# One written-out order of all steps replaced by another in an attention and Fourier-mixing kernel

## The chip, the core and the metric

The kernel runs on one core of a Trainium2 chip. The core has a matrix engine (PE, with its weight loads shown as PEld), a vector engine (DVE), a scalar engine (ACT), GpSimd (POOL) and a queue engine (SP) that here only starts transfers. Each engine works through its own list of instructions in the order in which the program gave them; between engines, semaphores hold an instruction back until what it reads is there and what it overwrites has been read. Transfers are started from SP, a few from ACT and POOL, and run on 16 DMA engines. The metric is the device time of the kernel in microseconds (us); lower is better.

## The reference, cut to what matters

Inputs are q, k and v of shape (4 batches, 8 heads, 768 positions, 64), and two matrices of 512x2048 and 2048x512. For each batch and head:

```python
k_rep = k.reshape(B, H, 12, 64, D).mean(axis=3)             # 12 blocks of 64 keys
gate = einsum('bhsd,bhnd->bhsn', q, k_rep), causal blocks only
sel = the 3 best blocks of each row, and its own block
scores = q @ k.T / 8, kept where the block is selected and the key is not later
attn_out = softmax(scores) @ v
```

The heads are put side by side to x of shape (4, 768, 512), and then

```python
mixed = real(fft(fft(x, axis=1), axis=2))
u = x + mixed
un = (u - mean(u)) / sqrt(var(u) + 1e-6)
out = u + maximum(un @ w_ch1, 0) @ w_ch2                    # 512 -> 2048 -> 512
```

## The kernel before, in words

Work on attention is cut into 16 pairs of heads, P = 0 to 15; batch b holds the pairs 4b to 4b+3. What follows works on a whole batch, in tiles of 128 positions.

The program is a list of steps, the string `ORDER` (line 112). A loop at its end (line 884) takes one word after another and calls the function that `WORK` (line 863) has for it. Since the tile framework runs with a manual schedule for all five engines, each engine's list is exactly the order in which these words put instructions on it. A word reads `name:numbers@place`. The place chooses which buffer of several a tile gets: for results of PE one of four pairs of PSUM banks (0 to 3), for loads one of two or three buffers in SBUF. A `~` ahead of the word gives its evacuation or copy to the other engine of two.

The steps that the prediction speaks of, by name, with their functions:

- `Lk`, `Lq`, `Lv` load k, q, v of a pair from SP (`load`, four transfers for k or q of pairs 7 and up at line 297, two before that at line 302, one for v at line 289). `LT` and `LF` load the Fourier tables fs_sb and fd_sb. `W`, `X` load the two matrices from POOL's queue. `Lc`, `Li` load the block indicators.
- `tk`, `tq` transpose k and q on PE, for pairs 0 to 6; `kb` and `qc` do it on DVE for the later ones. `ks`, `kh` sum blocks of keys (DVE); `kc`, `qc`, `qs` copy to 16 bits (`~qs` on ACT instead of POOL).
- `g` scores blocks on PE; `gt`, `gx`, `go`, `gl`, `gm` find the third-best block on DVE; for pairs from 7 on, `K` writes the mask into the operand on POOL.
- `s:P,i` computes the i-th of six tiles of scores on PE, `e:P,i` its exponential on ACT, `d:P,i` the causal diagonal on POOL.
- `vc` casts v (POOL, with `~` ACT), `v:P` multiplies with v on PE, `x:P` divides on DVE and writes x.
- `fs`, `fd`, `f` fold x by the symmetries of the Fourier sums (DVE); `y:b,h` and `m:b,kp` are the two Fourier products on PE. `ty` copies y on ACT (`~ty`: DVE), `tr` copies it reversed on DVE (`~tr`: ACT). `u` adds x and mixed (DVE). `xu` writes the 16-bit rows of u (ACT, `~xu`: DVE). `xt` transposes them on PE and `un` copies the result to unT on DVE, for batch 0; for the batches 1 to 3 `un` is two transposing transfers from SP (line 660). `bn`, `nv`, `nr` make the statistics.
- `w:b,it` multiplies unT with one of 16 column tiles of the first matrix, on PE; `r` is the relu that evacuates it (ACT, line 731, or with `~` DVE, line 729). `c` is the second product, `o` adds it to u (DVE), `od` stores.
- For batch 3 the second product is done by a seven-product scheme: `S` (`h_comb`) and `T` combine the operands on DVE, `p` multiplies, `po` adds to u.

A stage of one batch is laid among those of the next: the products `w` and `c` of batch b stand between the scores and exponentials of the pairs of batch b+1.

Of the kernel before, what the change touches and what calls it, by code (L numbers as in the profile page):

```python
# [117 lines left out]
gl:2 d:1,4 gt:3 vc:0 e:1,1 s:1,0@1 ~kc:4 tq:4@0 d:0,5 Lv:1@0 e:1,0 s:1,2@2 d:0,2 gx:3 v:0@3 Lk:5@2
e:1,2 gm:2@2 d:1,0 go:3 gl:3 gm:3@3 ~qc:4@1 s:1,5@1 s:2,4@2 vc:2 x:0 Lk:7@0 e:1,5 s:2,5@0 d:1,1
s:2,1@1 e:2,5@0 d:1,3 e:2,4 tq:5@3 fs:0,1 d:1,5 vc:1 g:4@0 e:2,1 qc:5@0 s:2,0@2 d:1,2 gt:4 e:2,0  # L120
s:2,2@3 Lq:6@0 d:2,4 d:2,5 s:2,3@1 fs:0,0 tk:5@0 e:2,2 qs:5 gx:4 v:1@2 go:4 Lv:3@1 ks:5 e:2,3 kb:7
kc:5 s:3,5@3 s:3,3@1 d:2,3 d:2,2 Lv:5@0 e:3,5@1 gl:4 s:3,4@0 d:2,1 e:3,3 x:1 g:5@3 qs:4 Lq:7@1
e:3,4 s:3,0@1 gt:5 d:2,0 s:3,2@2 d:3,3 fs:1,0 s:3,1@3 e:3,0 vc:3 gx:5 v:2@0 ks:7 e:3,1 d:3,4 d:3,5
# [12 lines left out]
s:7,5@2 w:0,14@1 Lv:7@0 e:7,5 e:7,4 kh:9 qc:9@1 Lq:10@1 s:7,1@2 X:0 r:0,10 go:8 ~r:0,14 w:0,0@3
e:7,1 d:7,4 gl:8 gm:8@0 K:8 s:7,3@0 ~r:0,0 g:9@1 e:7,3 w:0,15@2 bn:0,5 kb:10 w:0,2@3 r:0,15 X:1
fs:4,1 kc:8 ks:10 d:7,1 s:7,0@0 vc:7 v:6@2 gt:9 kc:9 gx:9 qs:9 w:0,4@1 ~r:0,2 e:7,0 go:9 d:7,3
w:0,9@3 gl:9 d:7,5 gm:9@1 ~r:0,4 d:7,0 K:9 s:8,2@0 Lk:11@1 x:6 v:7@1 e:8,2@0 bn:0,4 r:0,9 s:8,3@2
w:0,13@0 fs:5,0 e:8,3 x:7 s:9,0@3 fs:6,0 s:9,5@2 nv:0 w:0,7@1 e:9,5@1 ~r:0,13 e:9,0 nr:0 s:9,2@2  # L140
fs:4,0 r:0,7 kh:10 fs:7,1 s:8,1@0 fs:7,0 s:8,0@3 e:9,2 fs:6,1 c:0,0,0@1 fd:6,0 qc:10@0 e:8,0 fd:7,0
# [11 lines left out]
K:12 bn:1,1 e:10,2 g:13@0 fs:8,1 w:1,15@1 gt:13 s:11,1@0 d:10,2 ~r:1,15 w:1,13@3 d:10,5 e:11,1
d:10,1 ~r:1,9 vc:11 s:10,4@1 kb:14 r:1,13 d:11,0 w:1,0@0 Lv:12@0 vc:10 e:10,4 kb:15 d:10,3 s:11,5@2
s:12,0@3 ks:14 d:10,0 e:11,5 Lv:15@1 w:1,1@1 kc:13 d:10,4 d:11,5 od:0,2 gx:13 d:11,1 d:11,3 v:10@2
~r:1,1 r:1,0 qs:13 ~vc:12 go:13 s:12,3@0 w:1,8@1 fs:9,0 Lv:13@0 e:12,3@1 qc:14@1 gl:13 w:1,6@0
kh:14 ks:15 r:1,8 e:12,0 fs:8,0 w:1,7@1 bn:1,2 r:1,6 x:10 vc:13 s:12,1@3 r:1,7 s:12,2@0 gm:13@1
v:11@2 Lv:14@0 e:12,1 fs:10,1 K:13 od:0,4 e:12,2 g:14@1 w:1,4@3 gt:14 x:11 s:13,3@0 r:1,4 w:1,2@1
bn:1,5 bn:1,0 w:1,11@2 r:1,2 fs:10,0 fd:10,0 e:13,3@0 s:13,1@3 ~r:1,11 s:12,4@1 e:13,1 w:1,3@0
fd:10,1 gx:14 e:12,4 w:1,12@2 fs:11,0 r:1,3 nv:1 go:14 gl:14 nr:1 fs:11,1 s:13,0@3 kh:15 r:1,12  # L160
s:12,5@1 c:1,0,0@0 e:12,5 e:13,0 s:13,5@2 g:15@1 e:13,5 s:13,2@3 d:13,0 gt:15 c:1,1,0 d:13,5 e:13,2
fd:11,1 d:12,2 fd:11,0 kc:15 gx:15 w:1,14@2 gm:14@2 go:15 f:2,2 K:14 s:13,4@1 f:2,3 r:1,14 c:1,0,1
f:2,1 kc:14 gl:15 f:2,0 y:2,1@3 ~qs:15 y:2,0@2 d:13,3 ~tr:2,1 d:13,1 d:12,1 qs:14 c:1,1,1 e:13,4
tr:2,0 ty:2,0 d:13,4 c:1,4,0@1 d:12,4 o:1,1 d:12,0 ~ty:2,1 od:1,1 d:13,2 od:0,3 m:2,2@2 gm:15@3
o:1,0 m:2,0@3 K:15 od:1,0 v:13@0 u:2,0@0 c:1,4,1 u:2,2@1 d:12,3 pg:2 d:12,5 s:15,4@3 x:13 v:12@2
e:15,4@0 o:1,4 s:14,4@0 ~xu:2,2 s:14,1@3 e:14,4@1 un:2,2 c:1,5,0 fs:13,1 x:12 e:14,1 bn:2,4
s:15,3@0 d:14,1 d:15,4 s:15,0@2 e:15,3 ~xu:2,0 s:15,5@3 c:1,5,1 un:2,0 fs:13,0 e:15,0 d:15,3 e:15,5
m:2,1@0 s:15,2@2 u:2,1@4 c:1,2,0@3 e:15,2 bn:2,2 d:15,2 xu:2,1 d:14,4 s:14,5@0 s:14,2@2 o:1,5
un:2,1 c:1,2,1 e:14,5 d:15,0 bn:2,0 e:14,2 ~vc:15 c:1,3,0 od:1,4 s:14,0@1 c:1,3,1 e:14,0 ~vc:14
d:14,0 w:2,14@0 o:1,2 o:1,3 od:1,2 s:15,1@2 bn:2,1 od:1,3 w:2,1@1 e:15,1 od:1,5 ~r:2,14 d:15,1  # L170
# [749 lines left out]
```

## Time and profile before

| | |
|---|---|
| median of 3 runs | 285.47 us (283.56 to 288.51) |
| the profiled execution's own time | 282.36 us |
| span in its profile, first to last instruction | 280.6 us |
| PE busy | 270.4 us (96%) |
| DVE busy | 221.4 us (79%) |
| ACT busy | 166.3 us (59%) |
| POOL busy | 105.3 us (38%) |
| moved by DMA | 33.45 MB in 121280 packets |

The span is what the profile shows from the first instruction to the last; the rest of the time lies around it. Busy time of PE counts the pipelined matmuls with their modelled ends, so that neighbours overlap: two steps that follow without a gap start closer together than one matmul is long. The chain of work that ended last is followed back from the end, from each instruction to what released it or to its predecessor on the engine. A wait is idle time of an engine, put down to the semaphore that came last.

### The profile page before, as it was taken

The page shows a single profiled execution, that of the slowest core. Times are in us where ns is not written, and L with a number is a line of the kernel's source. Part 1 is how long each engine was busy: PE and PEld are TensorE (multiplying, and loading weights), DVE is VectorE, ACT ScalarE, POOL GpSimd, SP SyncE. Part 2 cuts the span into 40 slices and gives each one's busy share as a digit, 9 for nine tenths or more (in the row PEclk, how much of TensorE's full clock was granted, in tenths as well). Part 3 has the DMA queues.
Part 4 walks back from the last instruction along what each step waited for, and adds up shares of the span by engine and source line. Part 5 has one row for each costly group of instructions (what it writes and reads, how often), then busy time and mean ns, then how long its engine had stood idle before and what let it go on. Part 6 is the DMA issues. An engine that isn't in the chain of part 4 may idle for free.

```text
span 280.6 us, 6763 instructions
## 1 busy us (share of the span) xinstructions
PE 270.4 (96%) x2581; PEld 173.5 (62%) x2581; DVE 221.4 (79%) x683; ACT 166.3 (59%) x205; POOL 105.3 (38%) x273
## 2 busy tenths in 40 slices
...
GB/s 192 263 228 196 208 225 191 213 195 93 164 195 180 149 207 192 113 138 166 179 124 0 1 73 43 77 75 114 0 2 0 0 49 140 1 89 27 0 2 262
DMA packets 121280, 33.45 MB, mean 119 GB/s; under 512 B 113760, under 2 KB 118304, under 8 KB 121248
## 3 DMA queue, kind: packets, MB, share of 16 engines
...
q10 hardware_dynamic: 1712, 0.40, 0.7%
...
HBM read 28.55 MB, written 6.29 MB: 124 GB/s over the span
## 4 chain that ended last, share of the span: by engine, by line
PE 87%; DVE 4%; DMA 4%; SPq 2%; issue 1%; ACT 0%; ACTq 0%; DVEq 0%
PE c L738 22%; PE h L719 20%; PE h L721 10%; PE sc L457 7%; PE cw L794 7%; PE av L492 6%; PE yp L562 2%; SPq L297 2%; PE tp L317 2%; PE mx L595 2%; PE sc L452 2%; PE mx L596 2%; DMA fd_sb<-c_FD 2%; DMA nat<-in_q_dram 2%; PE g L378 1%; PE sc L464 1%
## 5 line engine op out<-in xcount | busy, mean ns | idle before, releaser
L474 ACT ACTIVATE pt<-sc 128x1024 f16<-128x1024 f32 (+1 forms) x96 | 83.8, 918 | 27.4 <-PE sc L457 22.3
L719 PE MATMUL h<-unT,w 128*128 128x512 f16 x256 | 84.8, 379 | 0.0
L721 PE MATMUL h<-unT,w 128*128 128x256 f16 x256 | 69.7, 272 | 0.0
L738 PE MATMUL c<-w_sb,hT 128*128 128x512 f16 x288 | 65.4, 379 | 0.0
L480 POOL TENSOR_SCALAR_AFFINE_SELECT pt<-pt 128x256 f16<-128x256 f16 x96 | 38.6, 427 | 44.1 <-ACT pt L474 38.7
L731 ACT ACTIVATE hT<-h 128x768 f16<-128x768 f32 x39 | 30.9, 810 | 38.1 <-PE h L721 38.1
L738 PEld LDWEIGHTS <-hT 128*128 128x128 f16 x288 | 27.8, 98 | 31.1
L719 PEld LDWEIGHTS <-w 128*128 128x128 f16 x256 | 25.0, 98 | 29.1 <-issue 0.9
L729 DVE TENSOR_SCALAR hT<-h 128x768 f16<-128x768 f32 x25 | 23.6, 946 | 10.0 <-PE h L721 9.9
L251 POOL TENSOR_SCALAR_AFFINE_SELECT qk<-mt 32x160 f16<-32x160 f16 x72 | 24.2, 357 | 15.3 <-DVE mt L429 13.3
L721 PEld LDWEIGHTS <-w 128*128 128x128 f16 x256 | 25.0, 98 | 3.6
L457 PE MATMUL sc<-qk 96*128 96x512 f16 (+3 forms) x144 | 26.5, 306 | 0.0
L492 PEld LDWEIGHTS <-pt 128*128 128x128 f16 x672 | 22.4, 97 | 2.4 <-POOL pt L480 0.4
L492 PE MATMUL av<-v,pt 128*128 128x65 f16 x672 | 23.3, 193 | 0.1
L744 DVE SCALAR_TENSOR_TENSOR u<-c,rs,u 128x512 f32<-128x512 f32 x18 | 13.0, 743 | 9.6 <-PE c L738 9.6
L457 PEld LDWEIGHTS <-qk 96*128 96x128 f16 x144 | 13.1, 97 | 9.2 <-issue 0.8
L614 DVE SCALAR_TENSOR_TENSOR u<-mx,x 128x512 f32<-128x512 f32 x22 | 14.3, 685 | 5.6 <-PE mx L596 5.4
L251 POOL TENSOR_SCALAR_AFFINE_SELECT qk<-q 64x768 f16<-64x768 f32 (+1 forms) x17 | 14.2, 834 | 8.3 <-ACT q L237 8.0
L248 DVE TENSOR_TENSOR x<-av,rcp 128x768 f16<-128x768 f32 x16 | 15.3, 958 | 0.5
L251 POOL TENSOR_SCALAR_AFFINE_SELECT v<-nat 128x768 f16<-128x768 f32 x12 | 10.9, 905 | 12.8 <-DMA nat<-in_v_dram 12.7
L452 PE MATMUL sc<-qk 64*128 64x512 f16 (+3 forms) x112 | 14.7, 306 | 0.8 <-ACT pt L474 0.6
L343 ACT CAST qk<-nat 64x768 f16<-64x768 f32 x18 | 14.9, 830 | 0.4
(132 smaller groups left out, 401.9 us busy)
## 6 DMA issues: line engine op xcount, KB each, us to landing
...
```

The source lines that it names most:

```text
L251: nc.gpsimd.affine_select(out=out, in_=in_, pattern=[[0, i] for i in n], base=0, channel_multiplier=0, compare_op=ALU.is_ge, fill=0.0)
L452: nc.tensor.matmul(ps[:, e, co:co + q1 - q0], qk[hs[e], 1, XW(P), 128 * jt:128 * jt + 128], qk[hs[e], 0, XW(P), q0:q1], start=(co == 0), s ...
L457: nc.tensor.matmul(ps[:, e, co:co + q1 - q0], qk[0:96, e, 1, 128 * jt:128 * jt + 128], qk[0:96, e, 0, q0:q1], start=True, stop=True)
L474: nc.scalar.activation(out=d["pt"][:, o:o + 2 * n].rearrange("p (e c) -> p e c", e=2), in_=d["sc", i][:, :, 0:n], func=AF.Exp, scale=0.125)
L480: nc.gpsimd.affine_select(out=dg, in_=dg, pattern=[[0, 2], [1, 128]], base=0, channel_multiplier=-1, compare_op=ALU.is_ge, fill=0.0)
L492: nc.tensor.matmul(av[:, e, 66 * st:66 * st + 65], pt[:, co:co + 128], vv[:, e, jt, 0:65], start=(cnt == 0), stop=(cnt == 20))
L719: nc.tensor.matmul(hp[:, 0:512], w1s, unT[:, dt, 0:512], start=(dt == 0), stop=(dt == NDT - 1))
L721: nc.tensor.matmul(hp[:, 512:768], w1s, unT[:, dt, 512:768], start=(dt == 0), stop=(dt == NDT - 1))
L729: nc.vector.tensor_scalar(out=hT, in0=hp, scalar1=0.0, scalar2=None, op0=ALU.max)
L731: nc.scalar.activation(out=hT, in_=hp, func=AF.Relu)
L738: nc.tensor.matmul(c_ps[b, g[0]][:, st - g[0], :], h_t[b, it][:, 128 * st:128 * (st + 1)], w2_sb[:, it, :], start=(it == 0), stop=(it == N ...
L794: nc.tensor.matmul(o, x, y, start=(i == 0 and W7_FIRST[n]), stop=(i == 7), skip_group_check=True)
```

## The change

The 1058 words of `ORDER` stay the same set of steps; their order is another, and so are 250 of the places behind `@`: 78 of `s`, 51 of `w`, 22 of `e`, 15 of `v`, the others in smaller numbers. Also changed is which steps carry the `~`:

- relus: 25 with `~` (on DVE) before, 18 after; ten get it and seventeen lose it
- `kc:0`, `kc:2` go to DVE and `kc:4` to ACT
- `qs:7`, `qs:9`, `qs:14` go to ACT, `qs:10` and `qs:12` to POOL
- `vc:4`, `vc:7`, `vc:9`, `vc:10`, `vc:13` go to ACT, `vc:14` and `vc:15` to POOL
- `tr:0,0`, `tr:1,0`, `tr:3,1` go to ACT, `tr:2,1` to DVE; `ty:0,1`, `ty:2,0`, `ty:3,1` go to DVE
- `xu:0,1` and `xu:2,1` go to DVE, `xu:2,0` and `xu:2,2` to ACT

In `h_comb` the two operands of a step are looked up only when that step runs, instead of all four ahead; this lets an `S` step stand ahead of a relu that it does not read, and changes no instruction.

The parts of the diff that the text below speaks of, with the lines between them left out:

```diff
 ORDER = """
...
-fs:2,0 e:4,4@0 fs:2,1 fd:2,1 e:4,1 Lv:4@1 gm:5@1 s:4,5@1 s:5,2@3 x:3 e:4,5 s:5,5@2 e:5,2@1 s:4,0@1
-Lk:9@2 d:4,5 fs:1,1 s:4,2@0 fs:3,1 e:4,0 fs:3,0 s:5,0@3 fd:2,0 fd:3,0 e:5,5 s:4,3@1 e:4,2 fd:3,1
-s:5,4@2 kh:7 f:0,1 e:5,4 s:5,3@0 f:0,0 LF:0 e:5,0 tk:6@2 f:0,3 e:4,3 Lk:8@1 f:0,2 y:0,0@3 ks:6 pg:0
-d:4,2 e:5,3 d:5,0 qc:7@1 W:1 y:0,1@1 kc:6 d:4,4 tr:0,0 Lq:8@2 g:6@0 d:4,0 ~tr:0,1 d:5,4 gt:6 vc:4
-m:0,2@2 ty:0,1 gx:6 W:0 s:5,1@0 ty:0,0 go:6 gl:6 u:0,2@0 g:7@1 d:5,3 qs:6 e:5,1 m:0,1@3 gt:7 ~vc:5
-d:5,1 m:0,0@2 u:0,1@1 d:4,1 xu:0,2 d:4,3 v:4@0 W:2 gm:6@2 xu:0,1 u:0,0@2 s:6,5@1 s:6,3@3 Lc:0
-e:6,5@0 e:6,3 xt:0,1@2 ~xu:0,0 s:6,1@1 un:0,1 xt:0,2@3 d:6,3 e:6,1 qs:7 xt:0,0@2 un:0,2 s:6,4@1
-un:0,0 s:6,2@3 e:6,4 kb:8 d:5,2 w:0,8@2 d:5,5 d:6,5 gx:7 w:0,5@1 go:7 x:4 r:0,8 e:6,2 gl:7 s:6,0@2
...
-d:8,5 od:0,1 g:11@3 Lq:13@2 g:12@0 ~qs:11 gt:11 m:1,1@2 gx:11 c:0,4,1 kc:12 go:11 gl:11 gm:11@3
-un:1,2 K:11 c:0,2,0@3 xu:1,0 o:0,5 gt:12 kb:13 c:0,3,0 od:0,5 u:1,1@2 d:9,0 un:1,0 d:9,1 d:8,0 vc:9
-s:11,4@0 s:11,2@2 o:0,4 c:0,3,1 xu:1,1 d:9,4 qc:15@0 un:1,1 pg:1 v:8@1 o:0,3 gx:12 c:0,2,1 e:11,4@0
...
+v:3@1 fs:2,1 Lv:4@0 W:0 e:4,0 gl:5 fd:2,0 LF:0 gm:5@1 ~qc:6@1 s:4,5@3 fs:1,0 s:5,0@0 x:3 e:4,5
+s:5,2@2 e:5,0@1 d:4,5 s:4,2@3 Lv:5@1 fs:1,1 s:5,5@1 e:4,2 fs:3,1 s:4,1@0 fs:3,0 fd:2,1 e:5,5 fd:3,0
+s:4,3@3 e:4,1 s:5,3@1 fd:3,1 f:0,0 e:5,2 tk:6@0 e:5,3 f:0,1 s:5,4@2 f:0,2 e:4,3 Lk:8@2 y:0,0@1
+f:0,3 ks:6 e:5,4 d:4,3 d:4,2 ks:7 d:4,0 ~tr:0,0 g:6@3 qs:6 y:0,1@2 gt:6 ty:0,0 d:5,4 gx:6 W:1
+s:5,1@3 Lc:0 ~tr:0,1 go:6 m:0,2@1 gl:6 W:2 kh:7 gm:6@2 kc:6 ~ty:0,1 Lk:9@1 d:4,1 ~vc:4 d:5,3
+m:0,0@0 u:0,2@0 d:5,5 e:5,1 d:5,0 d:4,4 m:0,1@2 u:0,0@1 xu:0,2 d:4,3 v:4@1 u:0,1@2 s:6,5@3 s:6,1@0
+e:6,5@0 e:6,1 s:6,0@3 s:6,3@2 ~xu:0,0 e:6,0 ~xu:0,1 xt:0,0@0 un:0,0 e:6,3 xt:0,1@3 xt:0,2@0 un:0,1
+kc:7 g:7@2 un:0,2 s:6,2@3 gt:7 s:6,4@0 e:6,2 gx:7 w:0,8@2 ~vc:5 go:7 x:4 d:6,2 d:5,1 w:0,1@3 r:0,8
+d:6,3 gl:7 d:5,2 gm:7@3 ~qs:7 pg:0 kb:8 d:6,0 w:0,6@1 Lq:8@2 K:7 bn:0,4 w:0,11@2 r:0,6 bn:0,2 r:0,1
+kb:9 Lq:9@0 v:5@1 r:0,11 ks:8 s:7,1@3 x:5 w:0,12@2 e:7,1@1 Li:0 ks:9 Lv:6@0 e:6,4 w:0,5@1 qc:8@1
...
+s:9,3@0 m:1,2@3 kc:12 kh:12 kh:11 go:10 gl:10 qc:12@1 c:0,5,1 u:1,2@3 e:9,3 Lk:14@1 ~qs:11 m:1,0@1
+d:9,3 qs:12 g:12@0 u:1,0@4 g:11@3 xu:1,2 c:0,4,1 Lv:10@1 d:9,0 d:9,4 od:0,0 gm:10@2 d:8,4 xu:1,0
+gt:11 d:9,2 c:0,2,0@1 d:8,0 un:1,0 gx:11 kc:11 go:11 o:0,4 gl:11 m:1,1@3 o:0,5 ~vc:10 gm:11@3
+c:0,3,0 gt:12 Lv:9@0 K:11 u:1,1@1 un:1,2 c:0,3,1 gx:12 xu:1,1 K:10 Lk:15@2 s:11,4@2 o:0,3 v:8@0
+s:11,2@3 x:8 e:11,4@0 c:0,2,1 un:1,1 e:11,2 d:11,4 kb:13 ~vc:9 s:10,2@2 o:0,2 s:11,3@0 kb:14 v:9@3
+Lq:13@1 e:11,3 go:12 ks:13 s:10,1@1 e:10,2@1 x:9 w:1,15@0 Lq:14@2 e:10,1 gl:12 s:11,0@2 gm:12@0
...
-        a11, a12 = h_t[b, i][:, 0:384], h_t[b, i + 8][:, 0:384]
-        a21, a22 = h_t[b, i][:, 384:S], h_t[b, i + 8][:, 384:S]
-        in0, in1 = ((a21, a22), (s[:, 0, :], a11), (a11, a21), (a12, s[:, 1, :]))[n]
+
+        def a(r, c):
+            return h_t[b, i + 8 * (c - 1)][:, 384 * (r - 1):384 * r]
+
+        in0 = (lambda: a(2, 1), lambda: s[:, 0, :], lambda: a(1, 1), lambda: a(1, 2))[n]()
+        in1 = (lambda: a(2, 2), lambda: a(1, 1), lambda: a(2, 1), lambda: s[:, 1, :])[n]()
         tt(s[:, n, :], in0, in1, ALU.subtract if n else ALU.add)
```

More of the change, by code (lines that the diff above doesn't have):

```diff
@@ L118 @@
[L118 to L123, printed above, removed]
@@ L136 @@
[L136 to L141, printed above, removed]
@@ L153 @@
[L153 to L170, printed above, removed]
@@ new lines @@
+qs:2 tk:4@1 e:1,1 gl:2 d:0,3 g:3@0 ks:4 Lq:5@2 d:1,0 kc:3 vc:0 tq:4@2 gt:3 kc:4 s:1,3@3 d:0,1
+gm:2@2 vc:2 ~qc:4@0 v:0@0 gx:3 Lv:1@0 go:3 e:1,3 d:1,2 gl:3 s:2,5@1 x:0 s:2,1@2 e:2,5@0 s:2,4@3
+e:2,1 Lv:3@1 g:4@1 fs:0,0 s:2,2@0 e:2,4 Lk:7@0 gt:4 d:2,1 s:1,5@2 d:1,3 tq:5@1 fs:0,1 e:1,5 gx:4
+d:2,4 e:2,2 s:2,0@3 d:1,1 s:2,3@2 qc:5@1 vc:1 e:2,0 tk:5@0 go:4 gm:3@3 d:1,5 v:1@1 e:2,3 d:2,5
+Lq:7@0 ks:5 gl:4 kc:5 d:2,3 s:3,2@3 x:1 d:2,0 s:3,0@2 vc:3 e:3,2@1 g:5@0 Lq:6@1 gm:4@0 d:2,2
+s:3,3@1 e:3,0 gt:5 qs:4 s:3,4@3 kb:7 LT:0 v:2@0 e:3,3 d:3,0 d:3,2 Lk:6@1 gx:5 e:3,4 d:3,3 s:3,1@2
@@ new lines @@
+vc:6 w:0,14@3 e:7,2 ~r:0,3 X:0 kh:8 kh:9 X:1 qc:9@0 s:7,5@0 w:0,9@1 r:0,14 d:7,3 bn:0,3 e:7,5 d:6,1
+kc:8 d:6,4 g:8@2 g:9@3 d:7,5 gt:8 d:6,5 w:0,10@0 fs:4,1 d:7,4 gx:8 Lk:11@2 w:0,15@2 go:8 gl:8
+r:0,10 gm:8@0 K:8 gt:9 ~r:0,9 v:6@0 r:0,15 bn:0,5 ~qs:9 s:7,0@3 x:6 w:0,7@1 d:7,1 e:7,0 gx:9
+w:0,0@2 r:0,7 nv:0 d:7,0 d:7,2 go:9 gl:9 s:8,3@0 r:0,0 gm:9@1 K:9 s:8,4@3 fs:5,1 w:0,4@1 ~vc:7
+fs:5,0 fs:6,0 e:8,4@0 fs:6,1 fd:6,0 w:0,13@2 r:0,4 kb:10 e:8,3 s:8,2@3 ~r:0,13 nr:0 w:0,2@1 kc:9
+v:7@0 r:0,2 e:8,2 s:8,1@2 Lq:10@1 x:7 c:0,0,0@1 e:8,1 ks:10 s:9,4@3 fs:7,1 Lk:12@1 fs:7,0 s:8,0@0
@@ new lines @@
+d:10,1 s:10,5@0 bn:1,4 g:13@2 e:10,5 s:10,4@3 r:1,13 d:10,5 gt:13 w:1,5@0 d:10,3 e:10,4 fs:9,0
+bn:1,1 s:11,5@2 d:10,4 w:1,7@1 r:1,5 ks:14 d:10,0 vc:11 e:11,5 qc:14@1 v:10@3 r:1,7 d:11,5 Lv:14@0
+gx:13 d:11,0 kc:13 od:0,5 qs:13 s:12,1@0 go:13 Lq:15@0 gl:13 w:1,1@2 x:10 bn:1,0 v:11@1 r:1,1 ks:15
+e:12,1@1 w:1,6@3 fs:10,0 od:0,2 ~vc:13 gm:13@1 kh:14 fs:8,0 K:13 x:11 s:12,0@2 Lv:15@1 r:1,6
+w:1,4@0 e:12,0 fs:11,1 fs:9,1 w:1,3@3 qc:15@0 fs:10,1 g:14@1 r:1,3 w:1,2@2 gt:14 r:1,4 fs:11,0
+fd:11,0 s:13,4@1 ~r:1,2 s:12,2@3 w:1,12@0 e:12,2 fd:11,1 fd:10,1 e:13,4@0 fd:10,0 w:1,0@2 kh:15
@@ new lines @@
+d:13,0 m:2,0@3 d:13,1 o:1,4 v:12@1 u:2,0@4 od:1,4 s:14,0@2 c:1,5,0 x:12 gl:15 gm:15@2 bn:2,1
+s:14,2@3 K:15 s:14,4@1 e:14,2@1 c:1,5,1 e:14,0 xu:2,0 d:14,2 m:2,1@3 o:1,5 pg:2 v:13@2 od:1,5
+u:2,1@0 kc:15 un:2,0 s:14,1@0 bn:2,2 e:14,4 c:1,2,0@3 ~xu:2,1 x:13 un:2,1 s:14,3@1 c:1,2,1 e:14,3
+e:14,1 d:14,3 vc:15 s:15,1@2 s:14,5@1 c:1,3,0 e:15,1@0 e:14,5 d:14,5 w:2,7@0 d:14,1 d:14,0 d:14,4
+c:1,3,1 ~r:2,7 bn:2,3 s:15,4@2 o:1,2 s:15,5@1 w:2,5@0 e:15,5 o:1,3 e:15,4 od:1,3 w:2,2@1 ~r:2,5
+od:1,2 s:15,2@3 ~r:2,2 s:15,3@2 w:2,15@0 fs:12,1 e:15,3 bn:2,0 e:15,2 fs:12,0 s:15,0@1 nv:2
```

74 lines of the change are left out of this document (38 added, 36 removed).

## The prediction

> **What bounds the kernel now.** I read the span on the page first, then the busy time of each engine in stretches cut at the starts of steps: 6.69 the first evacuation, 43.96 `y:0,0`, 58.48 `w:0,8`, 98.97 `y:1,0`, 123.17 `w:1,10`, 189.62 `w:2,14`, 237.85 `w:3,14`.
>
> ```profile
> span 280.6 us, 6763 instructions
> ```
>
> ```profile
> core 0: us, PE busy (x) PEld busy (x) DVE busy (x) ACT busy (x) POOL busy (x), PEclk, DMA share, GB/s
> 0.00:6.69 6.69, 5.17 (x21) 2.54 (x21) 1.75 (x11) 1.49 (x2) 1.59 (x17) 1.00 0.84 188
> 6.69:43.96 37.27, 34.34 (x564) 24.24 (x565) 32.53 (x131) 36.30 (x46) 17.86 (x35) 1.00 1.02 221
> 43.96:58.48 14.52, 12.21 (x190) 9.71 (x189) 13.01 (x44) 12.05 (x16) 9.60 (x19) 1.00 1.22 210
> 58.48:98.97 40.49, 40.49 (x364) 23.99 (x363) 39.17 (x132) 31.57 (x38) 25.53 (x64) 1.00 0.98 160
> 98.97:123.17 24.20, 24.20 (x234) 15.14 (x232) 21.32 (x69) 17.49 (x23) 10.75 (x29) 1.00 0.86 168
> 123.17:189.62 66.45, 66.45 (x562) 40.25 (x560) 49.23 (x152) 47.03 (x58) 31.60 (x81) 1.00 0.38 84
> 189.62:237.85 48.23, 48.23 (x359) 28.80 (x357) 35.28 (x85) 13.30 (x16) 8.35 (x29) 1.00 0.14 39
> 237.85:280.60 42.75, 39.30 (x297) 28.87 (x295) 29.08 (x65) 7.08 (x9) 0.00 (x0) 1.00 0.19 68
> ```
>
> From 58.48 to the last product PE never stands. Before that it does, and two other engines set the pace: ACT is busy 36.30 of 37.27 us up to `y:0,0`, and from there to `w:0,8` it is DVE with 13.01 of 14.52. The waits of PE say how much there is to win, and the chain of work shows that the end is PE work laid end to end.
>
> ```profile
> PE mx L595 <- DMA fd_sb<-c_FD: 1.8, 1, 1.8
> PE warmps L824 <- DVE zeros L821: 1.3, 1, 1.3
> PE g L371 <- ACT q L237: 0.9, 1, 0.9
> PE sc L464 <- DVE mt L429: 0.7, 1, 0.7
> PE sc L452 <- ACT pt L474: 0.6, 2, 0.4
> PE xt L652 <- ACT pt L474: 0.5, 1, 0.5
> PE tp L317 <- ACT pt L474: 0.3, 1, 0.3
> PE tp L317 <- DMA nat<-in_q_dram: 0.2, 1, 0.2
> PE g L371 <- DVE kr L329: 0.2, 1, 0.2
> ```
>
> ```profile
> 44.03 4.93 DMA fd_sb<-c_FD
> ...
> 115.57 0.86 PE sc L457 x4
> ...
> 118.16 1.28 PE av L492 x42
> ...
> 222.48 15.54 PE c L738 x72
> ...
> 258.82 18.35 PE cw L794 x168
> 277.19 0.48 DVE u L801
> ```
>
> Leaving out the warm-up's 1.3, the waits add to 5.2 us. PE's own work is the same set of instructions after the change. So an order without a single wait would win about 5.2 us of 280.6, under 2%; about 2% is what a measurement of this kernel can tell from no change, its three runs lying 1.7% apart. Any order can lose more than that. The rows also give the steps' lengths on PE: one `c` is 15.54/9 = 1.73 us, one `p` 18.35/21 = 0.87, one `v` 1.28, one full `s` 0.86/2 = 0.43, and one `w` 1.30 (258.82 less 238.02, over 16).
>
> **The change part by part.** First the work that changes engine.
>
> ```profile
> L731 ACT ACTIVATE hT<-h 128x768 f16<-128x768 f32 x39 | 30.9, 810 | 38.1 <-PE h L721 38.1
> L729 DVE TENSOR_SCALAR hT<-h 128x768 f16<-128x768 f32 x25 | 23.6, 946 | 10.0 <-PE h L721 9.9
> ```
>
> Seven relus net go from DVE to ACT, 7 x 0.946 = 6.6 us off DVE and 7 x 0.81 = 5.7 onto ACT; the other moved copies, about 0.8 to 1 us each half, make it some 8 us more on ACT and 5 less on DVE over the kernel. Nearly all falls where PE is the bound. In the stretch from 58.48 to 98.97 DVE has 39.17 of 40.49 us, the closest call there; it gets room, and ACT with 31.57 can take it. Worth nothing by itself, since PE already runs through; if that cover were gone, each us of overrun would cost one.
>
> *The start, to `y:0,0`.* ACT is full, so I compare what it has to finish before the place of `y:0,0` is free. Before, that is everything up to `e:5,0`; after, up to `e:5,3`. The same steps stand ahead except that `e:5,4`, `kc:0` and `kc:2` drop out and `e:5,3` and `kc:4` come in: one copy less.
>
> ```profile
> 41.03 4.71 ACT L474 ACTIVATE pt<-sc 128x1024 f16<-128x1024 f32 x5
> 46.70 1.02 ACT L237 CAST tr<-yp 128x768 f16<-128x768 f32 x1 [0.27 <-PE yp L562]
> 47.59 1.92 ACT L237 CAST ty<-yp 128x772 f16<-128x772 f32 x2
> ```
>
> An exponential takes 4.71/5 = 0.94, a copy of that size as long as the relu above, 0.81: ACT would be 0.8 us earlier. DVE must reach the two folds that `y:0,0` reads; ahead of them `ks:7`, `kh:7` and `kc:4` drop out, `kc:0`, `kc:2` and `qc:7` come in, about +0.8 us on an engine with 4.7 us of idle time in that stretch. The two offset each other: `y:0,0` at -0.8 to +0.8, I take -0.3.
>
> *From `y:0,0` to `w:0,8`.* `LF` now has one k load (`Lk:9`) and one v load fewer ahead of it in SP's queue, but `W:0` starts ahead of it on POOL. The load took 4.93 us from 44.03 and PE waited 1.8 for it. Issued by about 42 (an estimate: two loads earlier at some 1 us each), it lands by 46.9, before `m:0,2` wants it. What is late next? `m:0,2` needs both reversed copies, and both now are on ACT: after `y:0,0` starts, ACT does `e:4,3`, `e:5,4`, `tr:0,0`, `ty:0,0`, `tr:0,1`, which is 2 x 0.94 + 3 x 0.97 = 4.8 us. Before, `m:0,2` began 49.09 - 43.96 = 5.1 us after `y:0,0` with the DMA wait in it. The wait changes its name from the table to ACT and keeps nearly its length: 0.3 us won.
>
> From there DVE carries the way to `w:0,8`.
>
> ```profile
> 43.96 0.96 DVE L329 TENSOR_REDUCE kr<-tp 128x12 f32<-128x768 f32 x1
> 44.84 0.97 DVE L349 STREAM_TRANSPOSE q<-nat 128x768 f32<-128x768 f32 x1
> 45.73 0.99 DVE L239 CAST tr<-yp 128x768 f16<-128x768 f32 x1
> ...
> 55.41 0.88 DVE L642 TENSOR_SCALAR x<-u,nm 128x512 f16<-128x512 f32 x2
> 56.21 2.12 DVE L239 COPY unT<-xt 128x1024 f16<-128x1024 f16 x3
> ```
>
> Between `y:0,0` and `w:0,8` it loses `qc:7` (0.97) and `tr:0,0` (0.99) and gains `ks:7` (0.96), `kh:7` (0.2), `ty:0,1` (about 1) and a second `xu` (0.88): 13.01 + 1.1 = 14.1 us of work in what were 14.52. With the shorter DMA wait that fits to within half a us. PE reaches `w:0,8` with one more score tile (0.43) behind it. For the whole start I take -0.3 us; the bounds are -2.6, if the 1.8 and ACT's 0.8 both go and nothing takes their place, and +1.5, if the extra 1.1 of DVE and 0.4 of lost overlap come in full.
>
> *Pair 7's first scores.* Before, `g:7` has 17.8 us of PE work behind it until `s:7,2`; after, `s:7,1` follows with `s:6,2`, `s:6,4`, four `w` and `v:5` between: 0.8 + 5.2 + 1.3 = 7.3 us. In that time DVE has `un:0,2`, `gt`, `gx`, `go`, `x:4`, `gl`, `gm`, about 3.9 us, and then POOL the mask `K:7`, 2.69 by the row below: 6.6 us and two hand-overs. I put 0.4 us of waiting there, bounds 0 and 1.
>
> *Batch 1's transposed rows.* `w:1,15` needs all six transposing transfers of SP.
>
> ```profile
> 113.40 6.29 SPq L660 DMA_TRANSPOSE unT<-x  x4
> ...
> 120.37 4.38 SPq L297 DMA_DIRECT2D nat<-in_k_dram  x4
> ```
> ```profile
> 48.87 9.10 SPq L297 DMA_DIRECT2D nat<-in_q_dram  x4
> ```
> ```profile
> 64.34 2.69 POOL L251 TENSOR_SCALAR_AFFINE_SELECT qk<-mt 32x160 f16<-32x160 f16 x8 [0.71 <-DVE krb L248]
> ```
>
> Before, `un:1,0` and `un:1,1` stand side by side in SP's queue. After, SP issues `un:1,0`, `Lv:9`, `un:1,2`, the four transfers of `Lk:15`, and only then `un:1,1`. Counting from the start of `m:1,1`: `un:1,0` is through at about +0.7; `Lv:9` 0.6; `un:1,2` 2.8 (6.29/4 each, twice, rounded down for the wait in it); `Lk:15` about 3, an estimate below the 4.38 quoted, as fewer transfers are under way; `un:1,1` 2.8 and 1.2 more to land: +11.1. PE has after `m:1,1` (0.87) the steps `c:0,3,0`, `c:0,3,1`, `s:11,4`, `v:8`, `s:11,2`, `c:0,2,1`, `s:10,2`, `s:11,3`, `v:9`, `s:10,1`, 5.2 + 2.6 + 5 x 0.43 = 9.9, so it wants them at +10.8. I take 0.5 us of waiting, bounds 0 and 2. Behind `un:1,1` wait `Lq:13` and `Lq:14`, needed only some 10 us later.
>
> *The rest.* In batch 2 the same count leaves about 1 us of room (8.7 us of PE work, 7.7 for the transfers); batch 3 has the same fillers (`c:2`) as before. PSUM places are reused as fast as before: counting the PE work between the last product into a place and the next, 45 reuses have under 1.5 us against 50. At the end, `S` and `po` on DVE feed `p` with half a us to spare, and the last `p`, `po`, `od` are as before. For short waits that such counts miss I add 0.4, bounds 0 and 3.
>
> **The sum** is 280.6 - 0.3 + 0.4 + 0.5 + 0.4 = 281.6 us of span, a factor of 1.0036. The profiled execution's own time of 282.36 is 1.1% below the median of the three runs; the same factor on 285.47 gives **286.5**. The bounds together: -2.6 to +7.5 us, 282.8 to 293.1.
>
> [...] Transfers ran at 1.02 of the DMA engines' share up to 43.96 and 1.22 after it. [...]
>
> **The rivals.** *The start simply gets shorter*: the 1.8 of fd_sb and ACT's 0.8 go, DVE hides its extra work in its 1.5 us of idle time, nothing later waits: 278.0 us, or 282.8. For it: the table is loaded earlier and one copy leaves ACT. Against it: both reversed copies on ACT and DVE's 13.01 of 14.52. Chance 0.19, of which 0.06 over 2% faster (that would need more than all of PE's waits to go).
>
> *SP's queue takes the place of the old wait, on the slower side*: `Lk:15` holds `un:1,1` back. It decides from 10.8 us after `m:1,1` on; each us beyond is a us of idle PE. If the load takes the 9.10 us that `Lq:8` took, instead of 3, the rows land at +17.2 and PE stands 6.4 us instead of 0.5: 287.5, or 292.5. [...] Against it: DMA is at 0.86 there and not 1.22. Chance 0.17.
>
> *PE's clock drops.* PEclk is 1.00 in all stretches, the longest wait of PE being 1.8 us. In the warm-up nine matmuls of 512 columns took 3.64 us:
>
> ```profile
> 1.31 3.64 PE L824 MATMUL warmps<-zeros 128*128 128x512 f16 x9 [1.31 <-DVE zeros L821]
> ```
>
> That is 0.40 each, nearly twice the 0.216 of `c`'s 72. If a longer wait in the stretch after `y:0,0` brought that pace back for as long, it would cost 3.64 - 9 x 0.216 = 1.7 us: 283.3, or 288.2. [...] Chance 0.04.
>
> *The order does nothing it seems to*: all waits only change names, span 280.6, time 285.5; it lies inside the forecast, which with it has 0.60.
>
> **How the numbers follow.** Forecast 0.60 (283 to 290), shorter start 0.19, SP 0.17, clock 0.04. Faster by over 2% (below 279.8): 0.06. Slower by over 2% (above 291.2): most of SP's 0.17 and a little of the forecast's tail, 0.17. Within: 0.77. The range 281.5 to 292 takes in the shorter start and SP's price nearly in full.
>
> **What would show it.** Right: PE's wait for fd_sb gone and one for ACT's tr in its place; `w:0,8` within 1 us of 58.48; waits of PE at the first scores of pair 7 and at `w:1,15`; DVE busy some 5 us less, ACT 8 more. Wrong: `w:0,8` 2 us or more earlier or later, or a wait of several us in a place that the counts called free.

## The result and the profile after

The changed kernel takes **285.1 us** (median of 20 runs, 283.0 to 286.74). The kernel before took 283.64 us in 20 runs beside it (282.22 to 289.27). The ratio is **1.0051, 95% interval 1.0028 to 1.0074**: half a per cent slower, well inside the 2% within which the prediction put its 0.77. The profiled execution took 283.59 us.

The page's first line, and the waits of PE that it answers to (in order: what waited, what for, us in total, times, the longest). The three rows left out are 0.2 us each.

```profile
span 281.9 us, 6759 instructions
```

```profile
PE h L719 <- DMA unT<-x: 2.9, 2, 2.4
PE warmps L827 <- DVE zeros L824: 1.3, 1, 1.3
PE g L371 <- ACT q L237: 0.9, 1, 0.9
PE sc L464 <- DVE mt L429: 0.7, 1, 0.7
PE tp L317 <- DMA nat<-in_q_dram: 0.3, 1, 0.3
PE yp L562 <- ACT pt L474: 0.3, 1, 0.3
PE sc L452 <- ACT pt L474: 0.3, 1, 0.3
PE mx L595 <- ACT tr L237: 0.3, 1, 0.3
PE mx L595 <- DVE ty L239: 0.3, 1, 0.3
...
```

Add them without the warm-up: 6.6 us, where the kernel before had 5.2. That 1.4 is the 1.3 by which the span grew. The account is short: the 1.8 for fd_sb is gone, the other old waits are 0.3 longer in sum, and one new name, unT, costs 2.9. Everything else is the same work on PE, laid end to end in another order.

The busy time by stretches, cut at the same steps as before (`y:0,0`, `w:0,8`, `y:1,0`, then `w:1,15`, the first product of batch 1 in this order), shows where:

```profile
core 0: us, PE busy (x) PEld busy (x) DVE busy (x) ACT busy (x) POOL busy (x), PEclk, DMA share, GB/s
...
6.69:43.38 36.69, 33.90 (x566) 24.22 (x565) 33.32 (x130) 35.19 (x45) 18.68 (x36) 1.00 1.10 239
43.38:57.56 14.18, 13.07 (x197) 9.93 (x196) 13.24 (x49) 13.13 (x17) 5.55 (x12) 1.00 1.09 183
57.56:96.93 39.37, 39.37 (x356) 23.70 (x355) 33.67 (x111) 34.16 (x43) 22.94 (x64) 1.00 1.03 169
96.93:124.43 27.50, 25.12 (x239) 15.55 (x236) 24.12 (x91) 20.86 (x25) 12.65 (x33) 1.00 0.67 131
...
```

Before, PE was idle 2.31 of 14.52 us between `y:0,0` and `w:0,8`; now it is 1.11 of 14.18, with one score tile more in it. In the stretch up to `w:1,15` it stands 2.38 us, in what had been 24.20 us without a gap. DVE falls to 33.67 of 39.37 us in the middle stretch, where it had been at 39.17 of 40.49. Over the kernel DVE is busy 213.8 us (221.4 before), ACT 172.8 (166.3), POOL 96.5 (105.3).

SP's queue around the new wait, as the timeline has it (start, duration, queue and line, what):

```profile
107.92 2.17 SPq L750 DMA_DIRECT2D out_dram<-u  x1
110.20 2.61 SPq L660 DMA_TRANSPOSE unT<-x  x2
112.90 0.55 SPq L289 DMA_DIRECT2D nat<-in_v_dram  x1
113.52 2.93 SPq L660 DMA_TRANSPOSE unT<-x  x2
116.54 2.24 SPq L297 DMA_DIRECT2D nat<-in_k_dram  x4
118.88 2.50 SPq L660 DMA_TRANSPOSE unT<-x  x2
121.43 5.96 SPq L297 DMA_DIRECT2D nat<-in_q_dram  x8
```

and the end of the chain that leads to `w:1,15`:

```profile
120.17 4.22 DMA unT<-x
...
124.43 0.39 PE h L719
```

The pair of transposes at 118.88 is `un:1,1`. The four loads ahead of it at 116.54 are `Lk:15`, which before had stood far behind. The second half of `un:1,1` is issued from 120.17 and lands 4.22 us later; PE, which had run out of other work 2.38 us before, at 122.05, starts as soon as they are there.

### The profile page after: what moved, and what is told of

It reads as the page before. It is cut to its first block, busy times and chain, and to the rows that moved or that the text cites. A ratio compares the mean times of both kernels' runs of the same rounds, so it can differ in the third digit from the quotient of the medians.

```text
span 281.9 us, 6759 instructions
## 1 busy us (share of the span) xinstructions
PE 270.2 (96%) x2581; PEld 173.4 (62%) x2581; DVE 213.8 (76%) x678; ACT 172.8 (61%) x215; POOL 96.5 (34%) x268
## 3 DMA queue, kind: packets, MB, share of 16 engines
q1 hardware_dynamic: 115872, 28.43, 46.9%
## 4 chain that ended last, share of the span: by engine, by line
PE 79%; ACT 7%; DVE 6%; DMA 4%; issue 1%; SPq 1%; ACTq 0%
PE h L719 20%; PE c L738 19%; PE h L721 10%; PE cw L797 7%; PE sc L457 6%; ACT pt L474 5%; PE av L492 5%; PE yp L562 3%; DMA unT<-x 2%; PE tp L317 2%; DMA nat<-in_q_dram 2%; PE g L371 1%; DVE u L614 1%; PE sc L452 1%; PE mx L595 1%
## 5 line engine op out<-in xcount | busy, mean ns | idle before, releaser
L738 PE MATMUL c<-w_sb,hT 128*128 128x512 f16 x288 | 66.2, 379 | 0.0
L731 ACT ACTIVATE hT<-h 128x768 f16<-128x768 f32 x46 | 36.3, 810 | 35.9 <-PE h L721 35.9
L480 POOL TENSOR_SCALAR_AFFINE_SELECT pt<-pt 128x256 f16<-128x256 f16 x96 | 36.9, 409 | 54.8 <-ACT pt L474 48.1
L729 DVE TENSOR_SCALAR hT<-h 128x768 f16<-128x768 f32 x18 | 17.0, 950 | 13.6 <-PE h L721 13.6
L457 PE MATMUL sc<-qk 96*128 96x512 f16 (+3 forms) x144 | 27.1, 305 | 0.0
L251 POOL TENSOR_SCALAR_AFFINE_SELECT qk<-q 64x768 f16<-64x768 f32 (+1 forms) x15 | 12.4, 824 | 12.2 <-ACT q L237 7.6
L665 DVE BATCH_NORM_STATS2 bst<-u 128x6 f32<-128x512 f32 x22 | 14.8, 673 | 0.0
```

The lines of the kernel that those rows point to most:

```text
L251: nc.gpsimd.affine_select(out=out, in_=in_, pattern=[[0, i] for i in n], base=0, channel_multiplier=0, compare_op=ALU.is_ge, fill=0.0)
L457: nc.tensor.matmul(ps[:, e, co:co + q1 - q0], qk[0:96, e, 1, 128 * jt:128 * jt + 128], qk[0:96, e, 0, q0:q1], start=True, stop=True)
L480: nc.gpsimd.affine_select(out=dg, in_=dg, pattern=[[0, 2], [1, 128]], base=0, channel_multiplier=-1, compare_op=ALU.is_ge, fill=0.0)
L731: nc.scalar.activation(out=hT, in_=hp, func=AF.Relu)
L738: nc.tensor.matmul(c_ps[b, g[0]][:, st - g[0], :], h_t[b, it][:, 128 * st:128 * (st + 1)], w2_sb[:, it, :], start=(it == 0), stop=(it == N ...
```

## The experiments

Each kernel below keeps every instruction and changes only places in the order, or which engine has a step. A ratio is to the kernel before, with its 95% interval; small edits shift line numbers by one in some.

### Is it `Lk:15` ahead of `un:1,1`?

```diff
-un:1,2 c:0,3,1 gx:12 xu:1,1 K:10 Lk:15@2 s:11,4@2
+un:1,2 c:0,3,1 gx:12 xu:1,1 K:10 s:11,4@2
...
-c:0,2,1 un:1,1 e:11,2 d:11,4
+c:0,2,1 un:1,1 Lk:15@2 e:11,2 d:11,4
```

> The kernel after with one word moved: Lk:15 stands behind un:1,1 in SP's queue instead of ahead of it. Theory (SP's queue holds the transposed rows back): un:1,1, whose rows were ready at 115.6, is issued at about 116.5 instead of 118.9, the rows land 2.3 us earlier or more, PE's wait of 2.4 us at w:1,15 is gone, span 279.5 to 279.9, ratio to before about 0.996. Rival (the rows come late whatever stands ahead, because their second transfer took 3 us to land): the wait shrinks by under 0.5 us, span 281.4 to 281.9, ratio about 1.004.

Measured: 284.06 us, ratio 1.003 (0.9992 to 1.0068). The wait for unT before `w:1,15` is gone, and PE comes from `w:0,8` to `w:1,15` in 64.33 us instead of 66.87. But the gain does not reach the end. Another wait has come three `w` steps on, `PE h <- DVE hT` with 2.1 us, and DVE's timeline says who holds the eviction back (in brackets: idle time ahead of it, and what ended it):

```profile
126.17 0.98 DVE L320 STREAM_TRANSPOSE nat<-nat 128x768 f32<-128x768 f32 x1 [1.02 <-DMA nat<-in_k_dram]
...
129.01 0.98 DVE L348 STREAM_TRANSPOSE q<-nat 128x768 f32<-128x768 f32 x1 [1.54 <-DMA nat<-in_q_dram]
...
129.98 1.81 DVE L728 TENSOR_SCALAR hT<-h 128x768 f16<-128x768 f32 x2
```

The relu `r:1,10` (the first of the two at 129.98) stands in DVE's list behind `kb:15` and `qc:13`, which wait for two loads. Counted from `w:0,8`, `Lk:15` is now issued 2.9 us later than before the edit and `Lq:13` 0.3 us later, while PE is 2.5 us earlier. PE wants the PSUM place that this relu empties. So `Lk:15` was the cause of the first wait, and moving it made the next late loads the bound. The same run shows a clock that falls behind this wait, told below.

The mirror of it, on the kernel before: two loads put ahead of `un:1,1` there, the edit that should make the old order wait as the new one does.

```diff
+Lv:10@1 Lk:14@1 un:1,1 pg:1 v:8@1
-un:1,1 pg:1 v:8@1
...
-c:0,2,1 e:11,4@0 x:8 Lv:10@1 Lk:14@1 e:11,2
+c:0,2,1 e:11,4@0 x:8 e:11,2
```

> The kernel before with Lv:10 and Lk:14 moved ahead of un:1,1 in SP's queue. The rows of un:1,1 landed 2.25 us before PE wanted them. Theory (SP's queue): the two loads add 0.5 and 2.2 to 4.4 us, the rows land 0.5 to 2.7 us too late, PE waits so long at w:1,10, span 281.1 to 283.3, about 281.9. Rival (the room in front of w:1,10 or the queue's depth takes it up): span 280.6, no wait.

Measured: 286.61 us, ratio 1.0119 (1.0066 to 1.0172). SP's queue and PE's first product of batch 1:

```profile
118.77 2.90 SPq L296 DMA_DIRECT2D nat<-in_k_dram  x4
121.78 2.51 SPq L659 DMA_TRANSPOSE unT<-x  x2
```

```profile
126.41 0.38 PE L718 MATMUL h<-unT,w 128*128 128x512 f16 x1 [2.15 <-DVE mv L665]
```

PE stands 2.15 us where the kernel before had no gap. The profile puts the wait down to a small DVE instruction that ended at 126.15 and that `w` doesn't read; the last transposed rows landed at 126.32, 0.09 us before PE starts, so I read it as the transfer. The in-order queue does on the old order what it does on the new one. The profile's span, 284.1 us, is above the 281.1 to 283.3 that were expected: beside this wait, `w:0,8` came 0.6 us later, at 59.08.

### Where the gain went, followed one late load at a time

From here the changed order is edited further. First `kb:15` is moved behind the stuck relu, to where its result is wanted:

```diff
-s:11,0@2 gm:12@0 r:1,15 kb:15 s:10,0@3 K:12
+s:11,0@2 gm:12@0 r:1,15 s:10,0@3 K:12
...
-bn:1,0 v:11@1 r:1,1 ks:15 e:12,1@1
+bn:1,0 v:11@1 r:1,1 kb:15 ks:15 e:12,1@1
```

> The first experiment (Lk:15 behind un:1,1), and kb:15, the step on DVE that transposes this load, moved back to stand just ahead of ks:15. In the first experiment the wait at w:1,15 went, and PE waited 2.2 us two products later, for a relu on DVE. Theory (kb:15 waits for the load and holds DVE's queue, the relu of w:1,10 behind it): that second wait goes as well, nothing over 0.5 us is left between 115 and 140 us, and the kernel is 2 to 2.5 us faster than the changed one, ratio to before 0.993 to 0.998. Rival (DVE is simply late there, the load has nothing to do with it): the wait at the relu stays at about 2 us.

Measured: 283.95 us, ratio 0.9993 (0.996 to 1.0026). One wait is gone and the other has grown:

```profile
127.80 0.98 DVE L349 STREAM_TRANSPOSE q<-nat 128x768 f32<-128x768 f32 x1 [3.33 <-DMA nat<-in_q_dram]
128.90 1.81 DVE L729 TENSOR_SCALAR hT<-h 128x768 f16<-128x768 f32 x2
```

`qc:13` now waits 3.33 us, since its load `Lq:13` is issued behind `Lk:15`. PE still loses 1.9 us there. So `Lk:15` goes behind the q loads too:

```diff
-c:0,2,1 un:1,1 Lk:15@2 e:11,2 d:11,4
+c:0,2,1 un:1,1 e:11,2 d:11,4
...
-w:1,15@0 Lq:14@2 e:10,1 gl:12
+w:1,15@0 Lq:14@2 Lk:15@2 e:10,1 gl:12
```

> The order after, with Lk:15 behind Lq:14 and kb:15 just ahead of ks:15. Theory (loads on SP's queue set what arrives late): the load of nat for qc:13 is issued straight behind un:1,1, some 2.3 us earlier than with Lk:15 between them; DVE's wait of 3.33 us before qc:13 falls to about 1 us, PE's 1.9 us before w:1,13 to at most 0.5 us, and the span to about 279.5 us at a granted clock of 1.00 (281.1 with Lk:15 between), a ratio of 0.992 to 0.998. Rival (DVE itself is late there, whatever is loaded): PE still waits 1 us or more before w:1,13, and the ratio is 0.999 to 1.005.

Measured: 282.13 us, ratio **0.9934 (0.99 to 0.9967)**. DVE no longer waits for a load in front of the relu:

```profile
126.60 0.98 DVE L349 STREAM_TRANSPOSE q<-nat 128x768 f32<-128x768 f32 x1 [0.21 <-ACT hT L731]
...
127.76 0.96 DVE L729 TENSOR_SCALAR hT<-h 128x768 f16<-128x768 f32 x1
```

The span of this profile, 282.0 us, is not the 279.5 that was expected: its front waited longer for the q loads (1.05 us, and 1.02 more at the next such transposes, put down to ACT), so that `w:0,8` starts at 59.76. From `w:0,8` to the end it took 222.2 us, where the changed kernel took 224.3. As a second way to the same end, `qc:13` is put behind the relu, so that no late load stands in front of it at all:

```diff
-w:1,10@1 e:11,0 fs:8,1 qc:13@0 od:0,3
-kh:13 ~r:1,10 e:11,1
+w:1,10@1 e:11,0 fs:8,1 od:0,3
+kh:13 ~r:1,10 qc:13@0 e:11,1
```

> The run with Lk:15 behind Lq:14, and qc:13 put behind r:1,10 on DVE's queue, so that the eviction r:1,10 is held by no load at all. Theory: PE's wait before w:1,13 is gone (under 0.3 us) whatever the load does, the span is 279 to 280 us at a granted clock of 1.00, the ratio 0.990 to 0.998. Rival (DVE's own work ahead of r:1,10 is late): a wait of 0.7 us or more stays before w:1,13, put down to DVE with no DMA behind it.

Measured: **281.6 us, ratio 0.9928 (0.9898 to 0.9957)**, the fastest median of this study, and 0.7% faster than the kernel before. PE's list of waits has no row for unT or for a relu any more, and DVE takes the relu as soon as the product is there:

```profile
126.36 0.96 DVE L729 TENSOR_SCALAR hT<-h 128x768 f16<-128x768 f32 x1 [1.11 <-PE h L721]
127.23 0.97 DVE L349 STREAM_TRANSPOSE q<-nat 128x768 f32<-128x768 f32 x1
```

The changed kernel ran on the same chip beside these, as a control:

> The changed kernel itself, unchanged, on the same chip as the three runs beside it: a ratio of 1.003 to 1.007 to the kernel before, and PE's wait for unT before w:1,15 of 2 to 2.6 us in its profile again.

Measured: 284.65 us, ratio 1.0035 (1.0001 to 1.0069), with PE's wait for unT at 2.5 us. So the places of three words, `Lk:15`, `kb:15` and `qc:13`, all of them about loads and what stands behind them, are worth 1.1% of the time: 281.6 against 284.65.

### Batch 2's wait, and a store

In batch 2 the changed kernel's transposes come behind the store `od:1,5`, and PE waits 0.5 us before `w:2,7`. The store is moved behind them, first with `Lk:15` moved as in the first run, later with all three words in their last places:

```diff
-o:1,5 pg:2 v:13@2 od:1,5 u:2,1@0
+o:1,5 pg:2 v:13@2 u:2,1@0
...
-c:1,2,0@3 ~xu:2,1 x:13 un:2,1 s:14,3@1
+c:1,2,0@3 ~xu:2,1 x:13 un:2,1 od:1,5 s:14,3@1
```

> The first experiment, and od:1,5 moved behind un:2,1 as well. Theory (a store ahead of the transposing transfers holds them, un:2,0 took 4.1 us to issue behind it instead of 2.6): the rows of batch 2 land 1 to 2 us earlier, PE's wait at w:2,7 (0.5 us) is gone too, span 279.0 to 279.4. Rival (un:2,1 waits for its rows from DVE, not for SP): no change to the first experiment beyond 0.2 us.

> The run with qc:13 behind r:1,10, and the store od:1,5 behind un:2,1. Theory: the wait of 0.5 us before w:2,7 goes too, the span is some 0.5 us shorter than with the store in front, the ratio 0.989 to 0.997. Rival: the rows of the second batch have the room anyway and the ratio stays within 0.002 of the run without this edit.

Measured: 283.38 us, ratio 1.0004 (0.9968 to 1.0041), for the first; 281.99 us, ratio 0.9942 (0.9917 to 0.9967), for the second. Neither profile has a wait of 0.2 us or more before `w:2,7`. That does not make the store its cause: the first run above and the control, both with the store in its old place, have none either, nor has the run with the ratio 0.9928. SP needs 6.72 us for the four transposes in the changed kernel's profile and 5.52 in the first of these two runs, but 6.14 in the control, 6.17 with all three words moved, and 6.09 in the second run here. Beside the run without this edit, 0.9928, the second gains nothing that can be measured: the rival held. The first, too, is not clear of the run without it, 1.003, and its span of 283.1 us, with the relu's wait of 2.2 us in it, is far from the 279.0 to 279.4 that were expected.

One more edit was tried with `kb:15` and this store: `Lq:6` ahead of `Lk:7`, against a wait of PE for q loads in the front.

> The fifth experiment, with od:1,5 behind un:2,1 and Lq:6 ahead of Lk:7. In two runs PE waited 1.1 and 1.3 us at tq:6 for the load of q of pair 6, which stood behind the eight transfers of Lk:7 and Lq:7. Theory: those waits and the one at w:2,7 (0.3 to 0.7 us) are gone; another 0.5 to 1.5 us, ratio to before 0.988 to 0.995. Rival (the transfer engines are full up to 44 us, so another load comes late in its place, k of pair 7 at kb:7): no gain over the fifth experiment beyond 0.3 us.

Measured: 284.79 us, ratio 1.0033 (0.9998 to 1.0068). The rival was right: another step of the front is late in its place. DVE waits 1.88 us for the k load that `kb:7` transposes, and PE 1.8 us for DVE behind it.

```profile
PE h L719 <- DVE hT L729: 1.9, 1, 1.9
PE sc L452 <- DVE gt L420: 1.8, 1, 1.8
```

### The start

In the kernel before, the table fd_sb is issued behind `Lk:9`, and PE waits 1.8 us for it. Only that load is put behind it:

```diff
-s:5,5@2 e:5,2@1 s:4,0@1 Lk:9@2 d:4,5
+s:5,5@2 e:5,2@1 s:4,0@1 LF:0 Lk:9@2 d:4,5
...
-e:5,4 s:5,3@0 f:0,0 LF:0 e:5,0
+e:5,4 s:5,3@0 f:0,0 e:5,0
```

> The kernel before with one word moved: LF ahead of Lk:9, as the changed kernel has it. Theory (DVE carries the way from y:0,0 to w:0,8 and has only 0.3 us of idle time behind the 1.8 us wait for fd_sb): the wait of PE goes, w:0,8 comes 0.3 to 0.7 us earlier, span 279.9 to 280.3. Rival (the wait costs its length): span 278.8, 1.8 us less.

Measured: 286.83 us, ratio 1.0118 (1.0062 to 1.0174), and a profile with a span of 280.2. In the trace the wait for fd_sb is gone and `m:0,2` starts at 47.18 instead of 49.09, but `w:0,8` at 57.95 instead of 58.48: of 1.8 us 0.5 is left, the rest has gone to waits for DVE and ACT. That agrees with the theory that DVE carries this stretch. The time doesn't follow the profile: in four of its six runs the mean granted clock was 0.994 or lower, in the profiled one it was 1.00. The two at 1.00 had spans of 280.2 and 283.1 us, where the kernel before had a median of 281.65 at that clock, so a cost of the edit itself is not shown; why the clock fell so often, no run shows.

### Engines and order, each alone

The last pair takes the two halves of the change apart: the new order with the engines of before, so that each step has the `~` that it had, and the order of before with the new engines. Two places of the first:

```diff
-ks:7 d:4,0 ~tr:0,0 g:6@3 qs:6
+ks:7 d:4,0 tr:0,0 g:6@3 qs:6
...
-kc:6 ~ty:0,1 Lk:9@1 d:4,1 ~vc:4 d:5,3
+kc:6 ty:0,1 Lk:9@1 d:4,1 vc:4 d:5,3
```

> The changed order, but every step on the engine that it had before (the ~ marks of before). Theory (the moves to ACT are worth nothing by themselves where PE is the bound, and cost ACT time up to m:0,2): span within 1 us of the changed kernel, ratio to before 1.000 to 1.009. Rival (the new order needs DVE's 5 us of relief, since its evacuations stand closer to the reuse of their places): waits of PE for relus on DVE between 58 and 125 us, 2 us or more slower than the changed kernel, ratio 1.012 or more.

> The order before, with the engines of the changed kernel (its ~ marks). Theory (worth nothing by itself): span 280 to 281.6, ratio 0.997 to 1.005, DVE's busy time 5 to 7 us less and ACT's 6 to 8 us more. Rival (the order before was laid around its own division, so copies that ACT now does hold its exponentials back): 1.5 us or more slower, ratio 1.006 or more, waits of PE for ACT.

Measured: the new order with the old engines takes 291.19 us, ratio **1.0264 (1.0217 to 1.0311)**; the old order with the new engines 293.01 us, ratio **1.0335 (1.0277 to 1.0394)**. Each half alone costs about 3%, both together 0.5%. So the theory of both expectations, that the moves are worth nothing by themselves, failed, and the ratios are those of the rivals, although in the first the waits for relus on DVE come to only 0.6 us. PE's longest waits in the one (the other's stand below):

```profile
PE h L719 <- DMA unT<-x: 2.4, 1, 2.4
PE sc L457 <- POOL qk L251: 1.6, 2, 1.1
...
```

```profile
PE h L719 <- ACT hT L731: 3.1, 1, 3.1
PE mx L595 <- DMA fd_sb<-c_FD: 1.9, 1, 1.9
```

With the old engines POOL is late with the mask of pair 7, the wait that the prediction feared. That profile is 9.0 us longer than the changed kernel's: 3.3 of it up to `w:0,8`, 4.0 from there to `w:1,15` (1.1 of them the mask), and 1.7 behind it, where the clock fell, as the last section tells. With the new ones in the old order, a product waits 3.1 us for a relu that has come to ACT. An order written out by hand holds for one division of the work.

## Why the prediction was right, and where its terms were wrong

The forecast was a factor of 1.0036 and the measurement 1.0051; on the 283.64 us of the 20 runs, the predicted factor gives 284.7 against 285.1. The absolute 286.5 is higher because the 285.47 that it started from was a median of only three. The range and the side were right. But the sum came out by terms that were wrong in both directions, so that the nearness of the two factors is in part luck:

| step of the sum | predicted us | measured us |
|---|---|---|
| the start, to `w:0,8` | -0.3 (-2.6 to +1.5) | -1.35 |
| pair 7's first scores | +0.4 (0 to 1) | 0 |
| batch 1's transposed rows | +0.5 (0 to 2) | +2.4 |
| the rest | +0.4 (0 to 3) | +0.5, all in batch 2 (none in the control) |
| sum | +1.0 | +1.55 (span: +1.3) |

*The start.* -1.35 is 58.48 less 57.56, and 0.43 for the score tile more. Half of it is firm: from `y:0,0` to `w:0,8` took 14.17 or 14.18 us in eight profiles of the new order, against 14.52, with the tile more 0.77 won. The mis-sized step is "`m:0,2` needs both reversed copies". Its first matmuls need only the first:

```profile
45.10 1.02 ACT L237 CAST tr<-yp 128x768 f16<-128x768 f32 x1
45.99 1.03 ACT L237 CAST ty<-yp 128x772 f16<-128x772 f32 x1
46.87 1.02 ACT L237 CAST tr<-yp 128x768 f16<-128x768 f32 x1
```

```profile
47.27 0.28 PE L595 MATMUL mx<-fd_sb,tr 128*128 128x256 f16 x1
...
47.95 0.28 PE L595 MATMUL mx<-fd_sb,tr 128*128 128x256 f16 x1 [0.29 <-ACT tr L237]
```

It began 3.9 us after `y:0,0` and not 4.8, and the wait for ACT's copy, which the prediction named rightly, was 0.3. DVE was busy 13.24 us there and not the 14.1 counted. The other half, `y:0,0` itself, came 0.58 earlier, inside its bounds, but is no property of the order: it lay between 43.38 and 45.59 in eight profiles of the new order whose front is the same. The q loads of pairs 5 and 6 come just in time there, and waits for them, from none to 2.1 us in sum, come and go. In the control's profile, with 1.5 us of them, `w:0,8` starts at 59.14, later than the 58.48 of before.

*The table.* "Issued by about 42" and landed "by 46.9" were both wrong, without harm: it was issued at 34.31, in front of `Lv:5` and `Lk:8`, took 10.1 us instead of 4.93 (the row of DMA issues below), and landed at 44.4. `W:0` was issued at 36.38, within it.

```profile
fd_sb<-c_FD SPq DMA_DIRECT2D x1, 384.0 KB, 10.1
```

4.50 of the 10.1 us are the issue itself, which held SP's queue that long instead of 0.53, and from its end the table took 5.6 us to land, 4.4 before. In the run with the table early in the old order and `W:0` behind it, it took 7.0 us, 2.65 for the issue and 4.4 from its end. So the landing was 1.2 us longer with `W:0` issued within the load; since other loads differ too, that `W:0` made the 1.2 us is not shown, nor what held the issue.

*Pair 7.* `s:7,1` started at 64.05 straight behind `v:5`; POOL had the mask ready 0.65 us earlier. Of the moved copies it is `qs:7`, gone from POOL to ACT, that made room. With the old engines in the new order POOL does this copy first:

```profile
60.71 2.69 POOL L251 TENSOR_SCALAR_AFFINE_SELECT qk<-mt 32x160 f16<-32x160 f16 x8
```

```profile
63.48 1.70 POOL L251 TENSOR_SCALAR_AFFINE_SELECT qk<-q 64x768 f16<-64x768 f32 x2
...
66.09 2.69 POOL L251 TENSOR_SCALAR_AFFINE_SELECT qk<-mt 32x160 f16<-32x160 f16 x8
```

DVE had what the mask is made from 2.81 us after `w:0,8` in both profiles (60.37 and 63.63), so its relief, 33.67 busy of 39.37 us, did not decide here. PE stood 1.06 us for the mask with the old engines. At this row "Worth nothing by itself, since PE already runs through" failed: the prediction weighed the moves for DVE and ACT and left out POOL, whose busy time fell by 8.8 us.

*Batch 1's rows.* The mechanism, the place and PE's arrival were right: predicted +10.8 us after `m:1,1`, measured 122.05 - 111.09 = 10.96. The transfers came at +13.3 instead of +11.1, and the two terms mis-sized can be read from the rows of SP's queue above. `un:1,0` was through at +1.7 and not +0.7: the store `od:0,0`, left out of the count, held the queue for 2.17 us until 110.09, and ACT had the second half of its rows ready only at 110.39; what each made of the 1.0 is not shown. The last half took 3.0 us from the end of its issue to land, not 1.2. That goes with the loads again: counted from the start of its issue it landed after 4.2 us here and in the control, where `Lk:15` is issued just ahead of the pair, and after 2.5 in the first run above, where it is not. `Lk:15`, on the other side, took 2.24 instead of 3. The bound of 2 was exceeded. The rival in which this load takes 9.10 us didn't happen; its mechanism is what made the kernel slower all the same, at 2.4 us instead of 6.4.

*Batch 2* was said to have about 1 us of room. In the profile it had none, and PE waited 0.54 us; in the control, the same kernel, it did not wait. Its rows, too, were issued behind a store that the count had left out, but that the store made the wait is not shown.

*The clock rival*, with its 0.04, was underrated, as the last section tells: 15 of 32 runs of the kernel before and 17 of 32 of the changed one had a mean granted clock below 0.9965, so that it moves their times but not their ratio. That a longer wait brings the loss was the author's estimate: the last section has waits of about 2 us with a loss behind them and others without.
